# Two early loads of q asked for by ScalarE's queue instead of SyncE's, in a linear attention and gated MLP kernel

## The chip, the cores and the metric

The kernel runs on one core of a Trainium2 chip. The metric is the device time of one execution in microseconds, the median of several runs. The core has a matrix engine (TensorE, PE in the profile), VectorE (DVE), ScalarE (ACT), GpSimd (POOL), and SyncE (SP), which here does nothing but ask for transfers. ScalarE and GpSimd can ask for transfers too, each in a queue of its own. All transfers of the core run on its 16 DMA engines.

## The reference

Linear attention with decay in blocks of 64, and behind it a gated MLP with a spatial mix. B = 4, H = 8, S = 768, D = 64; the MLP has 512 inputs and 1024 hidden columns. Everything comes and goes as float32.

```
for b in range(nb):                        # blocks of 64 tokens
    intra = (qb @ kb.T * Dmask) @ vb       # Dmask = lam ** (i - j), i >= j
    inter = (qb * lam_pow) @ kv_state
    out[:, :, sl] = intra + inter
    kv_state = lam_block * kv_state + (kb * rev_pow).T @ vb
x = out as (B, S, 512)
h = relu(x @ w_in);  u, v = halves of h
v_n = (v - mean) / sqrt(var + 1e-6)
v_s = w_spatial @ v_n + b_spatial          # over the tokens
result = (u * v_s) @ w_out
```

## The kernel before, in words

The work goes in 12 steps, n = 0 to 11; three steps of 256 tokens make one batch element. Step n loads q, k and v of its 256 tokens for all 8 heads: one transfer of 512 KB each, which puts 128 partitions of 8 heads by 512 contiguous bytes in place. Each of q, k and v has three buffers, so step n takes the buffer of step n - 3.

The order of the work is written out by hand: the string ORDER lists tokens, and the loop at the end of the kernel turns each into the call of one helper. The last letter names the engine (T TensorE, D VectorE, A ScalarE, P GpSimd, S SyncE). Every engine works through its own tokens in the order of the string; waits between engines follow from the data. A token ahead of others on the same engine therefore holds these back for as long as it waits or works.

The tokens that matter here, with n the step:

- LK.n, LQ.n, LV.n load k, q and v. All go through the helper `load`, whose transfer is line 191 in the profile. `lam` loads the eight decay factors (L200). The argument 2 says all heads at once.
- WU runs matmuls on a constant tile, to keep TensorE busy (L212). LB, LN, LL, LX, LT make the decay tables from lam: a matmul (L217), a logarithm on ScalarE (L220), exponentials on ScalarE (L229 to L234). ScalarE loads a function table ahead of the logarithm and another ahead of the exponentials.
- KC.n and QC.n cast k and q to bf16 (L176 on VectorE, L178 on GpSimd). TK.n and TQ.n transpose them on TensorE (L328). EK.n copies the transposed k out of PSUM (L174), EQ.n does so for q and multiplies by its decay (L354).
- SC.n is the product of q and k (L369), MK.n masks it on VectorE (L373), VD.n multiplies v by its decay (L314), KV.n adds k times v to the state (L385), SS.n copies the state out (L174), AV.n forms the attention output (L406, L415), EX.n copies that out (L174).
- PV.n and PU.n are the two halves of the product with w_in (L438, L485). The later stages of the MLP are PW (L506), GB and GM (L511, L517), PO (L522).
- WI, WS and WO load the weights through GpSimd's queue, cast to bf16 on the way (L257, L262, L266). GT.0.1 makes GpSimd wait until k of step 1 has landed (L253), and WI.0, half of w_in, follows it. WI.1 stands behind half of VD.1 on GpSimd.

At the start SyncE's queue holds, in this order, k0, q0, k1, v0, q1, v1, k2, q2, v2, q3, k3, q4. ScalarE's queue holds lam alone; the next thing on ScalarE is the function table for the logarithm. On VectorE the casts, masks and products of the first steps come in the order QC.0, KC.1, EQ.0, VD.0 (two halves), MK.0 (two halves), EQ.1, MK.1. On TensorE the order is TQ.0, TK.0, TK.1, SC.0, KV.0.0, TQ.1, AV.0.0, SC.1.0, AV.0.1, SC.1.1, KV.0.1, KV.1.0, KV.1.1, AV.1.0, PV.0.1, AV.1.1, TK.2, TQ.2, with warm-up matmuls between.

Of the kernel before, what the change touches and what calls it, by code (L numbers as in the profile page):

```python
# [13 lines left out]


ORDER = """
LK.0.2.S lam.A pos.P LQ.0.2.S LK.1.2.S LV.0.2.S idn.P WU.-8.T LB.1.T msk.P LN.1.A LL.D LQ.1.2.S LX.A KC.0.2.P
LT.0.A LV.1.2.S QC.0.2.D mkc.A WU.29.T TQ.0.6.T LK.2.2.S TK.0.1.T GT.0.1.P WI.0.P KC.1.2.D EK.0.1.A EQ.0.6.D
WU.5.T TK.1.4.T LQ.2.2.S LT.1.A SC.0.1.5.T SC.0.0.1.T VD.0.0.D VD.0.1.D LV.2.2.S LT.2.A MK.0.0.1.D WU.7.T
KV.0.0.T QC.1.2.P MK.0.1.5.D EK.1.4.A WU.8.T TQ.1.2.T LQ.3.2.S SS.0.0.A AV.0.0.0.T EQ.1.2.D VD.1.0.P SY.0.0.A  # L20
# [564 lines left out]
```

## Time and profile before

| | |
|---|---|
| time, median of 3 runs | 148.21 us (147.82 to 151.35) |
| span of the profiled execution | 147.3 us |
| read from HBM, written | 24.77 MB, 6.29 MB |
| loads of q, k, v | 36, of 512 KB each |
| median time from issue to landing, k / q / v | 7.2 / 7.9 / 7.3 us |
| one issue in SyncE's queue, median for q | 1.74 us |
| half of w_in, from issue to landing | 8.9 and 10.1 us |
| lam's issue on ScalarE | 0.81 to 1.35 us |
| first function table on ScalarE | 1.38 us, 1.28 us long |

A line of the timeline gives the start, the duration, the engine, the source line, the operation with its output and inputs, and in brackets how long the engine had been idle before and what released it. "SPq" is an issue in SyncE's queue; its duration is the time for which the queue was held by that issue, and the data land later. In the table of stages each row is one stretch of time: its length, then for PE, PEld (the weight loads), DVE, ACT and POOL the busy time with the number of instructions, then the granted TensorE clock, the busy share of the DMA engines, and GB/s.

### The profile page before, as it was taken

Reading aid. Unit: us, or ns where it says so; the run is one execution under the profiler, and the core shown is the slowest. Engines: PE = TensorE matmul, PEld = TensorE weight load, DVE = VectorE, ACT = ScalarE, POOL = GpSimd, SP = SyncE. Lnnn points to the kernel's source line nnn. Section 1 sums busy time; section 2 is a strip of 40 time slices with the busy share of each in tenths; the row PEclk is TensorE's granted clock in tenths of the full one; section 3 lists DMA queues with packets and bytes.
Section 4 is the critical chain, followed back from the end, with each engine's and each line's share of the span. In section 5 each row is a group of like instructions: output and inputs, shape, how many; then the busy total and the mean of one; then the engine's idle time right before and its main releaser. Section 6 shows DMA issues by size and latency. Waiting matters only on the chain.

```text
span 147.3 us, 4874 instructions
## 1 busy us (share of the span) xinstructions
PE 138.3 (94%) x2075; PEld 90.7 (62%) x2075; DVE 101.1 (69%) x191; ACT 89.4 (61%) x167; POOL 70.5 (48%) x83
## 2 busy tenths in 40 slices
PE   6998698999999999899999899999999999999990
PEld 4786454768857768646656476556576565565540
DVE  1359606978996987799658499964598898738300
ACT  3979357968603876477994426676554567940370
POOL 7544660502269994864386924836735002034700
PEclk9999968999999999999999999999999999999998
DMA  3999999999999999999999998999993000070364
GB/s 87 302 290 260 270 256 258 217 238 293 276 287 283 291 268 176 304 259 95 277 324 180 200 237 260 312 200 346 255 219 97 2 7 0 0 268 21 142 259 169
DMA packets 54152, 31.25 MB, mean 212 GB/s; under 512 B 11634, under 2 KB 51058, under 8 KB 54130
## 3 DMA queue, kind: packets, MB, share of 16 engines
q1 hardware_dynamic: 51600, 28.05, 78.9%
q0 software_dynamic: 2384, 2.75, 11.0%
q8 instruction: 16, 0.26, 0.7%
q10 hardware_dynamic: 146, 0.13, 0.3%
q14 instruction: 6, 0.05, 0.1%
HBM read 24.77 MB, written 6.29 MB: 211 GB/s over the span
## 4 chain that ended last, share of the span: by engine, by line
PE 59%; DMA 19%; SPq 7%; POOL 5%; DVE 3%; ACT 2%; issue 2%; POOLq 0%; DVEq 0%; ACTq 0%
PE ps L506 15%; DMA q_in<-in_q_dram 14%; PE ps L522 12%; PE ps L485 11%; PE ps L438 10%; SPq L191 7%; DMA v_in<-in_v_dram 5%; POOL vd L314 3%; PE ps L415 2%; PE ps L369 2%; PE ps L385 2%; PE ps L498 1%; PE ps L328 1%; POOL qc L299 1%; PE ps L406 1%
## 5 line engine op out<-in xcount | busy, mean ns | idle before, releaser
L517 POOL TENSOR_TENSOR gT<-vsb,uT 128x384 bf16<-128x384 f32 x24 | 21.8, 920 | 31.1 <-DVE vsb L511 22.3
L506 PE MATMUL ps<-wt_sb,vn 128*128 128x384 bf16 x192 | 33.9, 326 | 0.0
L373 DVE TENSOR_TENSOR a_sb<-ps,m 128x1024 bf16<-128x1024 f32 x24 | 28.6, 1214 | 1.8 <-PE ps L369 1.4
L506 PEld LDWEIGHTS <-vn 128*128 128x128 bf16 x192 | 18.3, 98 | 11.9
L485 PE MATMUL ps<-xT,win_sb 128*128 128x256 bf16 x192 | 24.4, 273 | 0.0
L438 PE MATMUL ps<-win_sb,xT 128*128 128x512 bf16 x96 | 24.0, 387 | 0.0
L314 POOL TENSOR_TENSOR vd<-v_in,lv 128x512 bf16<-128x512 f32 x19 | 20.2, 1073 | 7.7 <-DMA v_in<-in_v_dram 7.7
L511 DVE TENSOR_TENSOR vsb<-ps,bsp 128x384 f32<-128x384 f32 x32 | 17.1, 549 | 8.6 <-PE ps L506 8.6
L522 PE MATMUL ps<-wout_sb,gT 128*128 128x512 bf16 x92 | 22.0, 379 | 0.0
L485 PEld LDWEIGHTS <-win_sb 128*128 128x128 bf16 x192 | 18.4, 98 | 4.9
L174 ACT ACTIVATE o_sb<-ps 128x512 f32<-128x512 f32 (+1 forms) x23 | 13.2, 587 | 11.1 <-PE ps L522 11.0
L174 ACT ACTIVATE xT<-ps 128x512 bf16<-128x512 f32 x22 | 15.2, 744 | 7.6 <-PE ps L415 7.6
L443 ACT ACTIVATE vh<-ps 128x512 bf16<-128x512 f32 x23 | 13.7, 597 | 9.1 <-PE ps L438 9.0
L453 DVE BATCH_NORM_STATS2 st<-vh 128x6 f32<-128x512 bf16 x24 | 16.3, 680 | 3.7 <-ACT vh L443 3.7
L299 POOL TENSOR_TENSOR qc<-q_in,lqn 128x512 bf16<-128x512 f32 x10 | 10.7, 1077 | 12.0 <-DMA q_in<-in_q_dram 9.0
L438 PEld LDWEIGHTS <-xT 128*128 128x128 bf16 x96 | 8.8, 98 | 9.6 <-issue 0.3
L522 PEld LDWEIGHTS <-gT 128*128 128x128 bf16 x92 | 8.8, 98 | 9.3
L443 ACT ACTIVATE uT<-ps 128x512 bf16<-128x512 f32 x20 | 11.7, 594 | 2.4 <-DVE mv L454 1.2
L178 POOL CAST kc<-k_in 128x1024 bf16<-128x1024 f32 x6 | 6.2, 1038 | 12.1 <-DMA k_in<-in_k_dram 7.8
L385 PE MATMUL ps<-vd,kc 64*64 64x64 bf16 x320 | 9.0, 194 | 2.6 <-ACT s_sb L174 1.0
L212 PE MATMUL ps<-warm 128*128 128x256 bf16 x61 | 9.7, 319 | 1.4 <-DVE warm L210 1.3
L174 ACT ACTIVATE kT<-ps 128x1024 bf16<-128x1024 bf16 x6 | 6.1, 1020 | 7.7 <-PE ps L328 7.2
(72 smaller groups left out, 178.0 us busy)
## 6 DMA issues: line engine op xcount, KB each, us to landing
k_in<-in_k_dram SPq DMA_DIRECT2D x12, 512.0 KB, 7.2
q_in<-in_q_dram SPq DMA_DIRECT2D x12, 512.0 KB, 7.9
v_in<-in_v_dram SPq DMA_DIRECT2D x12, 512.0 KB, 7.3
out_dram<-o_sb SPq DMA_DIRECT2D x23, 256.0 KB, 3.7
wsp_raw<-in_moe_w_spatial_dram POOLq DMA_DIRECT2D x2, 576.0 KB, 11.4
win_sb<-in_moe_w_in_dram POOLq DMA_DIRECT2D x2, 512.0 KB, 9.5
wout_sb<-in_moe_w_out_dram POOLq DMA_DIRECT2D x1, 512.0 KB, 8.9
bsp<-in_moe_b_spatial_dram SPq DMA_DIRECT2D x1, 384.0 KB, 6.7
```

The costliest lines, as they stand in the source:

```text
L174: nc.scalar.activation(out=o, in_=i, func=AF.Copy)
L299: vec(e).tensor_tensor(out=qc[n % NCA][:, :, :, o].rearrange("p u m d -> p (u m) d"), in0=q_in[n % NIN][:, 4 * o:4 * o + 4].rearrange("p u ...
L314: vec(e).tensor_tensor(out=vd[n % NCA].rearrange("p (o i w) m d -> p o i (w m) d", o=2, i=2)[o], in0=v_in[n % NIN].rearrange("p (o i w) m ...
L373: nc.vector.tensor_tensor(out=a_sb[n % NA][:, i].rearrange("p o w j x -> p (o w) (j x)"), in0=bank(b, 2).rearrange("p o (w y) -> p (o w) y ...
L438: nc.tensor.matmul(out=bank(b), lhsT=x[:, g % 2, c, c ^ (g // 2)], rhs=win_sb[:, g, DH:DFF], start=(g == 0), stop=(g == NCH - 1))
L443: nc.scalar.activation(out=o, in_=i, func=AF.Relu)
L453: nc.vector.bn_stats(out=st6[p2][:, t], in_=vh[p2][:, t])
L485: nc.tensor.matmul(out=pu[:, f2].rearrange("p (c x) -> p c x", c=2), lhsT=win_sb[:, g, f * P:(f + 1) * P], rhs=x[:, 4 * i + o:4 * i + 4 - ...
L506: nc.tensor.matmul(out=bank(b)[:, 0:HW], lhsT=vn[bb % 2][:, s, f * P:(f + 1) * P], rhs=wt_sb[:, s, i * HW:(i + 1) * HW], start=(s == 0), s ...
L511: nc.vector.tensor_tensor(out=vsb[(bb * 4 + f) % NVS][:, i * HW:(i + 1) * HW], in0=bank(b)[:, 0:HW], in1=bsp[:, i * HW:(i + 1) * HW], op=A ...
L517: vec(e).tensor_tensor(out=gT[bb % 2][:, f, cols], in0=vsb[(bb * 4 + f) % NVS][:, cols], in1=uT[bb % 2][:, f, cols], op=ALU.mult)
L522: nc.tensor.matmul(out=bank(b), lhsT=gT[bb % 2][:, f, t * P:(t + 1) * P], rhs=wout_sb[:, f, :], start=(f == 0), stop=(f == NCH - 1))
```

## The change

The loads of q of steps 0 and 1 leave SyncE's list and are put on ScalarE's, right behind the load of lam and ahead of everything else that ScalarE does. The aim is to have the first loads asked for from two queues at the same time. SyncE's queue then starts with k0, k1, v0, v1, k2, q2. No tile, size or computation changes; the lists of TensorE, VectorE and GpSimd stay as they are.

```
 ORDER = """
-LK.0.2.S lam.A pos.P LQ.0.2.S LK.1.2.S LV.0.2.S idn.P WU.-8.T LB.1.T msk.P LN.1.A LL.D LQ.1.2.S LX.A KC.0.2.P
+LK.0.2.S lam.A LQ.0.2.A LQ.1.2.A pos.P LK.1.2.S LV.0.2.S idn.P WU.-8.T LB.1.T msk.P LN.1.A LL.D LX.A KC.0.2.P
 LT.0.A LV.1.2.S QC.0.2.D mkc.A WU.29.T TQ.0.6.T LK.2.2.S TK.0.1.T GT.0.1.P WI.0.P KC.1.2.D EK.0.1.A EQ.0.6.D
```

## Prediction, made before the changed kernel was run

> **What bounds the kernel now.** I read the page first: busy shares, the 40 slices, the chain that ended last. TensorE is busy 94% of a 147.3 us span, and the transfer engines are full from the second slice on.
>
> ```profile
> PE 138.3 (94%) x2075; PEld 90.7 (62%) x2075; DVE 101.1 (69%) x191; ACT 89.4 (61%) x167; POOL 70.5 (48%) x83
> ...
> PEclk9999968999999999999999999999999999999998
> DMA  3999999999999999999999998999993000070364
> ```
>
> The reader should see two things: the DMA row is at 9 from 3.7 us to about 110 us, so a load cannot be made early without another coming late; and the TensorE clock drops once, near 20 us. Next I read the chain of waits, in order of time. Up to 22.6 us it is all loading; from 23.4 us it is TensorE, with only three later pieces of DMA.
>
> ```profile
> 6.81 1.74 SPq L191
> 8.59 1.74 SPq L191
> 10.37 12.22 DMA q_in<-in_q_dram
> 22.68 0.71 DVE qc L176
> 23.43 0.62 PE ps L328 x8
> ```
>
> So what counts for the end is when TQ.2 (the transposes of q of step 2, 23.43 us) can run, since behind it TensorE has hardly a gap. Then the timeline of the first 24 us, for the consumers of the first loads:
>
> ```profile
> 5.13 1.04 POOL L178 CAST kc<-k_in 128x1024 bf16<-128x1024 f32 x1 [0.43 <-DMA k_in<-in_k_dram]
> 6.90 0.69 DVE L176 CAST qc<-q_in 128x1024 bf16<-128x1024 f32 x1 [2.00 <-DMA q_in<-in_q_dram]
> 8.71 0.69 DVE L176 CAST kc<-k_in 128x1024 bf16<-128x1024 f32 x1 [1.11 <-DMA k_in<-in_k_dram]
> 10.52 1.29 DVE L314 TENSOR_TENSOR vd<-v_in,lv 128x512 bf16<-128x512 f32 x2 [0.52 <-DMA v_in<-in_v_dram]
> 12.37 1.03 POOL L178 CAST qc<-q_in 128x1024 bf16<-128x1024 f32 x1 [2.06 <-DMA q_in<-in_q_dram]
> 14.24 1.04 POOL L314 TENSOR_TENSOR vd<-v_in,lv 128x512 bf16<-128x512 f32 x1 [0.84 <-DMA v_in<-in_v_dram]
> ```
>
> Each waits for its transfer, so these are the landings of k0, q0, k1, v0, q1, v1: 5.1, 6.9, 8.7, 10.5, 12.4, 14.2 us, one every 1.8 us. The issues in SyncE's queue repeat every 1.78 us (5.03, 6.81, 8.59, 10.37): the queue runs at the pace of the transfers. The stage table shows that nothing is idle in it:
>
> ```profile
> 2.00:3.00 1.00, 1.00 (x6) 0.48 (x4) 0.00 (x0) 0.66 (x1) 0.94 (x3) 1.00 0.45 84
> 3.00:4.00 1.00, 1.00 (x5) 0.78 (x5) 0.01 (x1) 0.27 (x2) 0.88 (x4) 1.00 1.13 342
> 4.00:5.00 1.00, 1.00 (x6) 0.75 (x5) 0.89 (x3) 1.00 (x1) 0.68 (x1) 1.00 1.17 314
> 5.00:6.00 1.00, 1.00 (x7) 0.69 (x6) 0.00 (x0) 0.96 (x4) 0.86 (x1) 1.00 1.15 289
> ```
>
> The last two columns are the busy share of the transfer engines and GB/s: 289 to 342 GB/s from the fourth microsecond, with one queue in use.
>
> [...] one queue already fills the engines (289 GB/s). [...] No run here shows two load queues[...]. [...] granted clock 0.50 from 20 to 23 us, after TensorE was 0.25 to 0.52 busy between 16 and 19 us.
>
> **Part 1: what is removed and added in the queues.** Two issues leave SyncE's queue and two enter ScalarE's. Bytes, sizes and targets are the same. The gain in start is nil: the engines carry nothing before about 2.6 us either way (0.45 of the microsecond 2 to 3), and k0 alone then fills them. I price it at 0 to -0.2 us.
>
> **Part 2: the order of landing, worked out.** Unit: 1.8 us a load alone, 3.6 us while two share. k0 lands at 5.1, so its share of the stream starts at 3.3 on the scale of landings. q0 is asked for after lam's issue (0.81 + 0.54), some 0.6 us behind k0. k0 has a third done at 3.9; the rest at half rate takes 0.67 x 3.6 = 2.4: 6.3 us. q0 then lacks a third: 1.2 more, 7.5. k1, sharing with q1: 2.4 more, 9.9. q1: 1.2 more, 11.1. v0, now alone with 0.67 left: 1.2 more, 12.3. v1: 14.1. Against before: k0 +1.2, q0 +0.6, k1 +1.2, v0 +1.8, q1 -1.3, v1 -0.1. Bounds for v0: it cannot be later than the fifth landing, 12.4 (+1.9), and is 10.5 (0) if ScalarE's loads got nothing while SyncE's ran. I take +1.8. From v1 on the order and the bytes ahead are as before, so q2 keeps about 22.6 us. The half of w_in that GpSimd asks for at 9.39 waits for k1 and goes about 1.2 us later; this gives k2 and q2 a little, and its own first use (the matmuls of L438 at 19.42) moves later too.
>
> **Part 3: who waits for v0.** VectorE's list is KC.1, EQ.0, VD.0 (both halves), MK.0 (both), EQ.1, MK.1 (both). VD.0 at 10.52 moves to 12.3, and MK.0, 11.73 to 14.08, to 13.5 to 15.9. Behind it TensorE waits in program order: KV.0.0, TQ.1 (so that the earlier q1 buys nothing), AV.0.0 (14.01 to 15.8). EQ.1 follows MK.0 (14.18 to 16.0), then SC.1, MK.1, whose end goes from 18.05 to 19.85. AV.1.0 needs both masks. Before it ran at 18.87, 0.8 us after them, held by the state copies on ScalarE and by 0.76 us in which TensorE stood with no releaser. So after it runs between 19.85 (that slack used up) and 20.7 (all 1.8 passed on). From AV.1.0 to the end of TK.2 (22.83) TensorE took 3.96 us at the lowered clock, which gives 23.8 to 24.6 for the start of TQ.2, against 23.43 now, where it waits 0.6 us for q2. Shift at TQ.2: +0.4 to +1.2, middle +0.8.
>
> **Part 4: ScalarE.** Its table load (1.28 us, at 1.38) now stands behind two issues. The third issue of a queue cost 1.41 us in SyncE's, the second 0.56. Low end: 0.56 + 0.56, table load at 2.6, ready 3.9 against 3.71: +0.2 us. High end, [...]: ready at some 6.8, +3.1 us. I take about +1.0 (one of 0.56, one of 1.41). Behind it are the Ln, the Exps, the mask copies (end 8.03 to 9.0), then EK.0, which before waited 1.01 us for TensorE and now has its k0 later anyway. Even the high end puts EK.0's end at 12.1, ahead of the new MK.0 at 13.6, and EK.1 at 16.4 against EQ.1's end at 16.7. So it lies beside v0's delay: 0.
>
> **Part 5: how much reaches the end.** From 24 to 60 us TensorE has no idle time in the stage table (2.00 in each 2 us), so the shift goes through. Between 60 and 84 us it idles 0.41 + 0.06 + 0.07 + 0.38 = 0.9 us, for loads in the main; what of these isn't itself released later by the shifted work gives some back. Of +0.8 I let +0.7 remain: 148.2 + 0.7 = 148.9 us.
>
> **The rivals.** A, hidden: v0's delay ends in the wait for q2 (0.6 us) and the gaps of 0.9 us. For it: the sum of these exceeds 0.8. Against: the loads of the gaps follow the kernel's own releases. Time 148.2. B, faster: [...] the half-clock stretch is missed, or v0 is hardly late. Then the group of four L438 takes 0.97 for 1.66, TK.2 0.62 for 1.04, and with AV.1.1 some 1.2 us are saved; but TQ.2 still waits for q2, so at most the 0.6 us by which w_in's later transfer could bring q2 forward, and 0.2 of start: 147.4. C, slower: TensorE, starved from about 12 to 13.5 and 17 to 20 us, gets a second half-clock window of 3.4 us, in which half the work is lost (1.7 us), and ScalarE is at its high end, a further 0.5: 148.2 + 0.8 + 1.7 + 0.5 = 151.2, slower than before by 2%. For it: one such window is there already. Against: the warm-up matmuls fill the early gap.
>
> **How the numbers follow.** Forecast 0.55, A 0.2, B 0.1, C 0.15. The likeliest gives 148.9. The range goes from B less 0.3 for the spread of a time (147.82 to 148.21 in the two close runs), 147.1, up to C, 151.2, half of which lies beneath its own figure. Slower by 2% is 151.2 or more: most of C, 0.13. Faster by 2% is 145.2 or less, which no term here reaches: 0.03. Within: 0.84.
>
> **What would show it.** In the profile after: DVE's vd multiply at about 12.3 for 10.52, with the wait on v; GpSimd's cast of q1 near 11 for 12.37; the kc cast at 6.3; ScalarE's first table load between 2.6 and 5.5; TQ.2 at 23.8 to 24.6; DMA still at 9 in the second slice with no more GB/s. The prediction is wrong if v0 lands within 0.5 us of 10.5 (no equal sharing), if the rate in 3 to 14 us rises clearly over 290 GB/s, if TQ.2 moves and the end doesn't (Part 5), or if a new low-clock stretch shows.

## The result, and the profile after

The changed kernel takes 156.62 us (median; 155.68 to 157.28), the kernel before, with the later runs of it, 149.78 us (147.82 to 151.4). The ratio is 1.058, with a 95% interval of 1.048 to 1.068: slower by 5 to 7%, where 148.9 us was forecast with a range up to 151.2. (The ratios leave out slow executions, among them two of the kernel before at 151.4 us here and 10 of its 96 in four later series, at 155 to 157 us; none of these was profiled, so it isn't known whether they lose their time in the way that is shown below for the changed kernel.) The profiled executions span 147.3 us before and 154.0 us after.

The page of the changed kernel, busy shares and slices (one slice is 3.85 us):

```profile
PE 137.1 (89%) x2060; PEld 90.5 (59%) x2075; DVE 106.1 (69%) x191; ACT 89.9 (58%) x167; POOL 69.8 (45%) x83
...
PEclk9999998799999999999999999999999999999999
DMA  3999999999999969965999997999797000052364
```

TensorE does the same work (137.1 us busy for 138.3) in a span 6.7 us longer, so the loss is waiting. VectorE is busy 5.0 us longer than before with the same 191 instructions; some of them must have taken longer. The TensorE clock drops at a later place than before: it is 0.50 for 3.4 us from 25.5 us on, and was 0.50 for 3.4 us from 19.7 us on. The timeline of the changed kernel for the consumers of the first loads:

```profile
5.30 1.04 POOL L178 CAST kc<-k_in 128x1024 bf16<-128x1024 f32 x1 [0.65 <-DMA k_in<-in_k_dram]
7.56 0.69 DVE L176 CAST qc<-q_in 128x1024 bf16<-128x1024 f32 x1 [2.60 <-DMA q_in<-in_q_dram]
10.10 0.69 DVE L176 CAST kc<-k_in 128x1024 bf16<-128x1024 f32 x1 [1.85 <-DMA k_in<-in_k_dram]
11.97 1.03 POOL L178 CAST qc<-q_in 128x1024 bf16<-128x1024 f32 x1 [0.27 <-DMA q_in<-in_q_dram]
12.50 1.65 DVE L314 TENSOR_TENSOR vd<-v_in,lv 128x512 bf16<-128x512 f32 x2 [1.11 <-DMA v_in<-in_v_dram]
```

The order k0, q0, k1, q1, v0 came as forecast. The only number here that matters later is k1: 10.1 us instead of 8.7. The chain of waits of the changed kernel, the two stretches in which TensorE doesn't carry it (start, duration, what):

```profile
10.24 14.16 DMA q_in<-in_q_dram
24.49 0.70 DVE qc L176
25.25 0.82 PE ps L328 x8
...
32.04 2.03 POOL vd L314 x2
34.11 0.25 PE ps L385 x5
...
60.14 5.07 DVE gT L517
65.21 0.61 DVE st L453
```

The first stretch: q2 is there at 24.4 us for 22.6, and v2's multiply by its decay (VD.2) runs on GpSimd at 32.0 us. The second: one multiply on VectorE (GM, L517) takes 5 us. Neither was in the prediction. How late the work is after these, by the start of the same instruction before and after, in us:

| | before | after | later by |
|---|---|---|---|
| SC.2, scores of step 2 (L369) | 25.71 | 29.20 | 3.5 |
| KV.2, first use of v2 (L385) | 29.00 | 33.10 | 4.1 |
| first PU behind it (L485) | 29.71 | 34.69 | 5.0 |
| the multiply GM.0.3.0 (L517) | 54.94 | 60.05 | 5.1 |
| state product behind it (L385) | 59.65 | 67.78 | 8.1 |
| end of the span | 147.3 | 154.0 | 6.7 |

So 5 us come before 35 us, 3 more at 60 us, and 1.4 are given back.

**Why v2 is late.** The timeline of GpSimd, before: its request for half of w_in, the cast of k2, its request for w_spatial, VD.2.

```profile
9.39 0.92 POOL L257 DMA_DIRECT2D win_sb<-in_moe_w_in_dram  x1
...
19.53 1.04 POOL L178 CAST kc<-k_in 128x1024 bf16<-128x1024 f32 x1 [2.42 <-PE ps L415]
20.51 0.79 POOL L262 DMA_DIRECT2D wsp_raw<-in_moe_w_spatial_dram  x1
...
25.76 2.04 POOL L314 TENSOR_TENSOR vd<-v_in,lv 128x512 bf16<-128x512 f32 x2 [3.54 <-DMA v_in<-in_v_dram]
```

The same after:

```profile
10.78 0.92 POOL L257 DMA_DIRECT2D win_sb<-in_moe_w_in_dram  x1
...
18.61 1.04 POOL L178 CAST kc<-k_in 128x1024 bf16<-128x1024 f32 x1 [1.34 <-issue]
19.59 0.78 POOL L262 DMA_DIRECT2D wsp_raw<-in_moe_w_spatial_dram  x1
...
32.02 2.04 POOL L314 TENSOR_TENSOR vd<-v_in,lv 128x512 bf16<-128x512 f32 x2 [10.73 <-DVE a_sb L373]
```

The request for w_in, gated by k1, goes 1.4 us later, and that for w_spatial 0.9 us earlier: w_in's first packet now goes at 14.93 us for 13.12, when k2 is nearly through (whole at 16.02 us for 19.38), so the cast of k2 no longer waits for it and starts 0.9 us earlier. (The releaser of the last line is only the event that came last by the profile; the landing below tells what VD.2 waited for.) In the trace each load adds 16 counts to its semaphore, and the first use comes behind the last of them (v2's at 31.87 us, VD.2 at 32.02). I take each count for the part of the load that one of the 16 transfer engines has done. Landing of the 16 parts, in us:

```
        15 parts           last part
k2  before  17.99-18.36   19.38
    after   15.53-16.02 (all 16)
q2  before  19.79-20.19   22.59
    after   19.69-20.27   24.40
v2  before  23.59-25.45   25.61
    after   23.74-25.98   31.87
```

Fifteen parts of q2 and v2 come as before, within 0.1 and 0.5 us. One part is behind, by 1.8 us more for q2 and 6.3 us more for v2. (That it is the same engine's each time is assumed; the records don't name the engine.) What it runs into shows in the table of stages in half microseconds, the last column being GB/s. Before:

```profile
24.00:24.50 0.50, 0.50 (x4) 0.20 (x2) 0.41 (x1) 0.12 (x1) 0.00 (x0) 1.00 1.16 344
24.50:25.00 0.50, 0.50 (x4) 0.22 (x3) 0.50 (x2) 0.04 (x1) 0.00 (x0) 1.00 1.16 342
```

After:

```profile
24.00:24.50 0.50, 0.00 (x0) 0.00 (x0) 0.01 (x1) 0.47 (x1) 0.00 (x0) 1.00 1.22 297
24.50:25.00 0.50, 0.00 (x0) 0.00 (x0) 0.50 (x1) 0.00 (x0) 0.00 (x0) 1.00 1.17 220
```

At 340 GB/s SyncE's queue has the engines nearly alone (653 packets per us for 10 of GpSimd's queue, 24.0 to 25.0 us before); at 220 they share with the packets of GpSimd's queue (106 and 112 per us, 24.5 to 25.0 us after), which are cast on the way. Before, w_in's packets are through between 24.0 and 25.0 us but for some 10 per us, and w_spatial's first one goes at 24.99 us; in that gap the engine that is behind can catch up. After, w_spatial's first packet goes at 24.09 us, most of the gap is gone, and the engine does its part of v2 beside w_spatial. That it catches up in the gap isn't seen directly, but the rates fit. A load is 1024 packets of 512 bytes, 64 to a part if the parts are equal. Alone (10.5 to 12.5 us), SyncE's queue moves 575 packets per us in the kernel before, beside w_in (20.5 to 23.5 us) 138 of its own and 137 of GpSimd's, beside w_spatial (25.2 to 31.0 us) 107 and 107; its stream falls from 290 to 70 and 53 GB/s. At a sixteenth of these rates 64 packets take 1.8, 7.4 and 9.6 us, by estimate. v2's last part came 3.02 us after q2's before, so by the same estimate the engine was alone for some 1.4 us of it, and 7.47 us after it in the changed kernel, which leaves 0.5 us at most.

### The profile page after: what moved, and what is told of

The parts are those of the page before. It is cut to its first block, busy times and chain, and to the rows that moved or that the text cites. A ratio compares the mean times of both kernels' runs of the same rounds, so it can differ in the third digit from the quotient of the medians.

```text
span 154.0 us, 4860 instructions
## 1 busy us (share of the span) xinstructions
PE 137.1 (89%) x2060; PEld 90.5 (59%) x2075; DVE 106.1 (69%) x191; ACT 89.9 (58%) x167; POOL 69.8 (45%) x83
## 4 chain that ended last, share of the span: by engine, by line
PE 68%; DVE 10%; DMA 9%; SPq 6%; ACT 2%; issue 2%; POOL 1%; DVEq 0%
PE ps L506 19%; PE ps L522 13%; PE ps L438 11%; PE ps L485 10%; DMA q_in<-in_q_dram 9%; SPq L191 6%; DVE gT L517 3%; PE ps L369 3%; PE ps L415 3%; DVE a_sb L373 2%; PE ps L328 2%; PE ps L385 2%; PE ps L406 2%; PE ps L498 1%; POOL vd L314 1%
## 5 line engine op out<-in xcount | busy, mean ns | idle before, releaser
L517 POOL TENSOR_TENSOR gT<-vsb,uT 128x384 bf16<-128x384 f32 x24 | 21.8, 917 | 40.1 <-DVE vsb L511 31.4
L314 POOL TENSOR_TENSOR vd<-v_in,lv 128x512 bf16<-128x512 f32 x19 | 19.6, 1043 | 18.5 <-DVE a_sb L373 10.7
L485 PE MATMUL ps<-xT,win_sb 128*128 128x256 bf16 x192 | 24.4, 273 | 0.0
L522 PE MATMUL ps<-wout_sb,gT 128*128 128x512 bf16 x86 | 21.4, 379 | 0.4 <-issue 0.2
L485 PEld LDWEIGHTS <-win_sb 128*128 128x128 bf16 x192 | 18.4, 98 | 4.9
L385 PE MATMUL ps<-vd,kc 64*64 64x64 bf16 x320 | 8.9, 193 | 6.2 <-DVE s_sb L176 2.9
L385 PEld LDWEIGHTS <-kc 64*64 64x64 bf16 x320 | 7.4, 109 | 8.3 <-issue 7.3
L174 ACT ACTIVATE s_sb<-ps 128x256 bf16<-128x256 f32 x16 | 6.1, 382 | 8.3 <-PE ps L385 7.4
L415 PE MATMUL ps<-a_sb,vd 64*64 64x128 bf16 x384 | 10.5, 217 | 0.3 <-DVE a_sb L373 0.3
```

Source lines behind the costliest of these rows:

```text
L174: nc.scalar.activation(out=o, in_=i, func=AF.Copy)
L314: vec(e).tensor_tensor(out=vd[n % NCA].rearrange("p (o i w) m d -> p o i (w m) d", o=2, i=2)[o], in0=v_in[n % NIN].rearrange("p (o i w) m ...
L385: nc.tensor.matmul(out=pkv[row(o), u], lhsT=kc[n % NCA][row(c), u, m, o, :], rhs=vd[n % NCA][row(c), 4 * o + u, m, :], start=new and u == ...
L485: nc.tensor.matmul(out=pu[:, f2].rearrange("p (c x) -> p c x", c=2), lhsT=win_sb[:, g, f * P:(f + 1) * P], rhs=x[:, 4 * i + o:4 * i + 4 - ...
L517: vec(e).tensor_tensor(out=gT[bb % 2][:, f, cols], in0=vsb[(bb * 4 + f) % NVS][:, cols], in1=uT[bb % 2][:, f, cols], op=ALU.mult)
L522: nc.tensor.matmul(out=bank(b), lhsT=gT[bb % 2][:, f, t * P:(t + 1) * P], rhs=wout_sb[:, f, :], start=(f == 0), stop=(f == NCH - 1))
```

## The experiments

All compute the whole result. Where GpSimd is to be delayed, a token DL.n makes it fill a scratch tile of n columns that nothing reads (0.77 us for 768). Three theories stood at the start. Theory 1: w_in later, so k2 and w_spatial earlier, so the slowest part of q2 and v2 late. Theory 2: two queues of loads as such leave one transfer engine behind. Theory 3: v0 late, TensorE starved, half clock.

**e1: the changed kernel, with w_spatial asked for as late as before.**

```
-WS.1.P AV.1.1.3.T ...
+DL.768.P WS.1.P AV.1.1.3.T ...
```

> The changed kernel with 0.8 us of idle work on GpSimd ahead of its first request for w_spatial. Theory 1 (in the changed kernel k2 lands earlier, so GpSimd asks for w_spatial 0.9 us earlier, its packets close the gap in which SyncE's queue had the transfer engines alone, and the slowest engine's part of q2 and v2 comes late): the request goes from 19.6 to 20.4 us as before the change, q2 is there by 23.2 us for 24.5, v2 by 27 for 32.0, and the time comes down to 149 to 152 us. Theory 2 (two load queues at once leave one transfer engine behind the others, whatever w_spatial does) and theory 3 (v0 late, TensorE starved, half clock): 155 us or more, as the changed kernel.

Measured: 149.42 us, ratio to the kernel before 1.005 (1.001 to 1.009). Timeline of GpSimd and, below, the half microseconds of e1:

```profile
19.93 0.77 POOL L547 IOTA dly<- 128x768 int32 x1
20.66 0.79 POOL L262 DMA_DIRECT2D wsp_raw<-in_moe_w_spatial_dram  x1
...
25.74 2.04 POOL L314 TENSOR_TENSOR vd<-v_in,lv 128x512 bf16<-128x512 f32 x2 [3.37 <-DMA v_in<-in_v_dram]
```

```profile
24.00:24.50 0.50, 0.50 (x4) 0.24 (x3) 0.50 (x2) 0.50 (x1) 0.00 (x0) 1.00 1.14 338
24.50:25.00 0.50, 0.50 (x3) 0.15 (x2) 0.47 (x2) 0.50 (x2) 0.00 (x0) 1.00 1.16 344
```

So 0.8 us of idling on GpSimd takes away all but 0.5% of the loss. The gap at 24 to 25 us is back, v2 is whole at 25.59 us (and q2 at 22.02), and the multiply of L517 takes 0.55 us. Both queues of loads and the late v0 are still there, so theories 2 and 3 can hold for no more than the 0.5%, which is near the noise (e4 below has 0.4% with v0 on time).

**e2: the kernel before, with only w_in asked for later.** All loads stay in SyncE's queue in the old order.

```
-... GT.0.1.P WI.0.P KC.1.2.D ...
+... GT.0.1.P DL.768.P DL.512.P WI.0.P KC.1.2.D ...
```

> The kernel before with 1.4 us of idle work on GpSimd ahead of its first request for w_in, so that this goes out at 10.8 us as in the changed kernel; all loads stay in SyncE's queue. Theory 1: k2 lands some 2 us earlier, w_spatial is asked for earlier, v2 is there only after 30 us, 153 to 157 us. Theories 2 and 3: no second load queue and v0 on time, so 148 to 150.5 us.

Measured: 157.01 us, 1.0575 (1.0493 to 1.0657), the whole loss. GpSimd in e2:

```profile
9.27 1.38 POOL L547 IOTA dly<- 128x768 int32 x2
10.61 0.92 POOL L257 DMA_DIRECT2D win_sb<-in_moe_w_in_dram  x1
...
17.95 1.04 POOL L178 CAST kc<-k_in 128x1024 bf16<-128x1024 f32 x1 [0.96 <-PE ps L385]
18.92 0.79 POOL L262 DMA_DIRECT2D wsp_raw<-in_moe_w_spatial_dram  x1
...
31.93 2.04 POOL L314 TENSOR_TENSOR vd<-v_in,lv 128x512 bf16<-128x512 f32 x2 [11.30 <-DMA v_in<-in_v_dram]
```

Here the profile names v2's transfer as what VD.2 waited for. q2 is whole at 24.40 us and v2 at 31.78, as in the changed kernel (24.40 and 31.87): the later request for w_in is enough, with one queue and v0 on time.

**e3 and e4: the order without the second queue, and q0 alone in it.**

```
e3  -LK.0.2.S lam.A pos.P LQ.0.2.S LK.1.2.S LV.0.2.S ... LQ.1.2.S
    +LK.0.2.S lam.A pos.P LQ.0.2.S LK.1.2.S LQ.1.2.S LV.0.2.S ...
e4  -LK.0.2.S lam.A pos.P LQ.0.2.S LK.1.2.S LV.0.2.S ...
    +LK.0.2.S lam.A LQ.0.2.A pos.P LK.1.2.S LV.0.2.S ...
```

> All loads in SyncE's queue, in the order in which they land in the changed kernel (k0, q0, k1, q1, v0, v1); v0 lands at 12.4 us, but k1 at 8.7, so that w_in is asked for at 9.4 as before. Theory 1: the shift of v0 alone, 148 to 151 us. Theory 2: as before, 148 to 150. Theory 3: all of the loss, 154 to 157 us.

> Half of the change: q0 in ScalarE's queue, q1 in SyncE's where it was. k0 lands near 6.3 us, k1 near 8.9, v0 near 10.5. Theory 1: w_in is asked for at some 9.6 us, 148 to 151 us. Theory 2: a good part of the loss, 151 to 155. Theory 3: 148 to 150.

Measured: e3 149.33 us, 1.0053 (0.9998 to 1.0107); e4 149.32 us, 1.0039 (0.9992 to 1.0087). In both k1 comes in time, w_in is asked for at 9.36 and 9.42 us, w_spatial at 20.50 and 20.51, and v2 is whole at 25.40 and 25.67. One load of q in ScalarE's queue did no measurable harm here, where k1 wasn't pushed back. In e3 v0 is late (12.27 us) about as in the changed kernel, in e4 on time (10.52 us); the times don't tell the two apart, so no cost of a late v0 is seen.

**e5: the changed kernel, with w_in freed from k1.** Its gate is q0 instead, and a delay puts the request at 9.20 us.

```
-... GT.0.1.P WI.0.P KC.1.2.D ...
+... GT.1.0.P DL.1024.P WI.0.P KC.1.2.D ...
```

> The changed kernel, with its first request for w_in at the time that it had before (9.4 us for 10.8): GpSimd waits for q0 in place of k1 and then does 1.1 us of idle work. Both load queues stay. Theory 1 (w_in later, so k2 earlier, so w_spatial earlier, so v2's last part late): k2 lands near 19 us again, w_spatial is asked for at 20.4 or later, v2 is there by 27 us, 148 to 151 us. A rival, that the two queues are needed for the loss too: 153 us or more.

Measured: single times of 148.92, 148.88, 153.04 and 157.57 us; no ratio can be given. In the profiled one (148.92) w_spatial is asked for at 20.30 us and v2 is whole at 27.45. With the request at its old time the loss can be avoided, but not in each execution. That v2 is caught in some and not in others is argued from this profile; the other times have none. How far the engine is behind counts too: in e7 below w_spatial is asked for earlier than here, at 20.07 us, and v2 is still whole at 25.14 us; there q2's last part was there at 20.73 us, here at 23.52.

**e8: half the delay of e2** (DL.640, 0.65 us, in the same place).

> The kernel before with 0.7 us of idle work ahead of the first request for w_in, half of that of the changed kernel. If the loss grows with the lateness: about 152 us. If it is a cliff, since k2 either comes ahead of w_in's packets or is caught in them: either 148 to 149.5, or 156 to 157. Theory 1 names the sign in the trace: k2's landing goes with w_spatial's request, and the time with v2's last part.

Measured: 150.88, 156.94, 157.09 and 159.83 us, no ratio. In the profiled one (150.88) 15 parts of k2 are there by 15.8 us and the last at 19.1; w_spatial goes at 20.23, v2 is whole at 29.0. One of the four lies near 151, three near 157 and above: more like a cliff than a slope. In this profile the multiply of L517, at 58.5 us, takes 0.55 us; the collision that is told of below, under e6, isn't there. That it makes the step from 151 to 157 is possible, and not shown.

**e9: the kernel before, with w_spatial asked for earlier.** w_in and all loads are untouched; the cast of k2 (KC.2) now stands behind the two requests.

```
-... KV.1.1.T KC.2.2.P AV.1.0.3.T ... / WS.1.P AV.1.1.3.T EV.0.1.5.A QC.2.2.D GT.2.1.P WS.0.P TK.2.2.T ...
+... KV.1.1.T DL.1024.P DL.768.P WS.1.P GT.2.1.P WS.0.P KC.2.2.P AV.1.0.3.T ... / AV.1.1.3.T EV.0.1.5.A QC.2.2.D TK.2.2.T ...
```

> The kernel before with its loads and w_in untouched; only the two requests for w_spatial are taken ahead of the cast of k2 on GpSimd and set by idle work to about 18.9 and 19.8 us, where the delayed w_in had put them (20.5 and 21.4 before). q2 has its usual 22.5 to 23.2 us, since w_in is as before. If the early w_spatial alone makes v2's last part late: v2 after 29 us and 151 to 156 us, less than the 157 of the delayed w_in since q2 is on time. If it takes w_in's lateness too: v2 by 27 us, 148 to 150 us.

Measured: 158.27 us, 1.0589 (1.048 to 1.0698), more than expected. GpSimd and TensorE in e9:

```profile
18.83 0.79 POOL L262 DMA_DIRECT2D wsp_raw<-in_moe_w_spatial_dram  x1
...
31.69 2.04 POOL L314 TENSOR_TENSOR vd<-v_in,lv 128x512 bf16<-128x512 f32 x2 [10.10 <-DMA v_in<-in_v_dram]
```

```profile
25.94 0.64 PE L369 MATMUL ps<-qT,kT 64*64 64x128 bf16 x32
...
32.79 0.31 PE L385 MATMUL ps<-vd,kc 64*64 64x64 bf16 x8 [3.49 <-POOL vd L314]
```

q2 is whole at 22.82 us and the scores of step 2 start at 25.94, as before the change (25.71); v2 is whole at 31.55 us, and TensorE waits for VD.2. The cast of k2 runs at 20.54 us for 19.53, which can account for no more than these 0.2 us. So the time of w_spatial is enough, and v2 alone makes the delay.

**e10: the changed kernel, kept warm while q2 is missing.** Twelve warm-up matmuls (WU.12) ahead of TQ.2.

> The changed kernel with twelve warm-up matmuls between the transposes of k2 and q2, where TensorE stood 2.5 us for q2 and then ran at half clock from 25.5 to 28.9 us. If the half clock is a part of the loss of its own: the granted clock stays at 1.00, the score matmuls of step 2 start at some 28 us for 29.2, and 0.5 to 1.7 us come back, 155 to 156. If v2, which lands after 31 us, decides behind it anyway: 156 to 157.5, no gain.

Measured: 156.50, 157.55, 159.49 and, once, 149.33 us. TensorE, and one microsecond of the stages, in the profiled execution (156.50 us):

```profile
26.62 0.64 PE L369 MATMUL ps<-qT,kT 64*64 64x128 bf16 x32
...
32.43 0.31 PE L385 MATMUL ps<-vd,kc 64*64 64x64 bf16 x8 [2.45 <-POOL vd L314]
```

```profile
27.00:28.00 1.00, 1.00 (x24) 0.51 (x13) 0.96 (x3) 0.98 (x2) 0.00 (x0) 1.00 1.16 219
```

The column before the last two is the granted clock: 1.00, where the changed kernel has 0.50. The scores move 2.6 us forward (29.20 to 26.62), KV.2 only 0.7 (33.10 to 32.43), and the span stays (154.8 us). In this execution, half clock and the late q2 lie in the shadow of v2. The one of 149.33 us has no profile.

**e6 and e7: the multiply of L517.** In the changed kernel it takes 5.15 us, against 0.55. VectorE and GpSimd at that place in the changed kernel:

```profile
60.05 5.15 DVE L517 TENSOR_TENSOR gT<-vsb,uT 128x384 bf16<-128x384 f32 x1
```

```profile
59.89 1.04 POOL L299 TENSOR_TENSOR qc<-q_in,lqn 128x512 bf16<-128x512 f32 x1
60.89 1.03 POOL L314 TENSOR_TENSOR vd<-v_in,lv 128x512 bf16<-128x512 f32 x1
61.89 1.03 POOL L299 TENSOR_TENSOR qc<-q_in,lqn 128x512 bf16<-128x512 f32 x1
62.89 1.03 POOL L314 TENSOR_TENSOR vd<-v_in,lv 128x512 bf16<-128x512 f32 x1
63.89 0.90 POOL L517 TENSOR_TENSOR gT<-vsb,uT 128x384 bf16<-128x384 f32 x1
```

The multiply starts 0.16 us behind the first of five operations of GpSimd and ends 0.41 us behind the last. GpSimd has no gap between the five. In e2 it is the same with four of them: the multiply takes 4.12 us, from 0.20 us behind the start of the first (62.14 us) to 0.42 us behind the end of the last (66.04 us). That GpSimd's operations held the multiply back is read from these times; the record names no releaser. Before, the multiply ran at 54.94 us, and GpSimd had a gap there, from 54.99 to 57.19 us, waiting for q7:

```profile
54.94 0.55 DVE L517 TENSOR_TENSOR gT<-vsb,uT 128x384 bf16<-128x384 f32 x1
```

```profile
57.19 1.04 POOL L299 TENSOR_TENSOR qc<-q_in,lqn 128x512 bf16<-128x512 f32 x1 [2.20 <-DMA q_in<-in_q_dram]
```

With the program 5 us later, q7 has already landed and the gap is missing. e6 and e7 move this one multiply to GpSimd (GM.0.3.0.D to GM.0.3.0.P), in the changed kernel and in the one before.

> The changed kernel with one multiply (L517, batch 0, third group, first half), which took 5.15 us on VectorE at 60 us while GpSimd ran five operations without a gap, moved to GpSimd's list. If this wait is a second part of the loss of its own: the span between the transposes of step 3 and the end is as before the change, and 1.5 to 3 us come back, 153.5 to 155 us. If it is only idle time that would have been spent in another wait: within 0.7 us of the changed kernel, 156 to 157.

> The same move in the kernel before, as a control; there the multiply took 0.55 us on VectorE with GpSimd idle beside it. It costs GpSimd 0.9 us ahead of two multiplies that wait for q7 anyway: 148 to 149.3 us.

Measured: e6 151.85 us, 1.021 (1.008 to 1.034); e7 148.76 us, 1.0055 (1.002 to 1.009). v2 is still late in e6 (31.32 us). The stage from 64 to 68 us, in which TensorE loses the time, in the changed kernel and then in e6:

```profile
64.00:66.00 2.00, 0.86 (x6) 0.40 (x4) 1.97 (x4) 0.62 (x2) 0.79 (x1) 1.00 1.15 305
66.00:68.00 2.00, 0.22 (x15) 0.22 (x17) 1.97 (x6) 0.00 (x0) 0.00 (x0) 1.00 0.79 207
```

```profile
64.00:66.00 2.00, 2.00 (x77) 1.42 (x77) 1.33 (x3) 1.30 (x4) 1.56 (x3) 1.00 1.15 318
66.00:68.00 2.00, 1.95 (x59) 1.24 (x50) 1.65 (x2) 1.15 (x2) 1.75 (x3) 1.00 0.61 154
```

TensorE works 1.08 of 4 us there, and 3.95 with the multiply moved. By the profiled spans the collision costs 3.1 us (154.0 - 150.9), by the medians, which come from different series, 4.8 (156.62 - 151.85): about half of the loss. In the kernel before the move gains nothing.

**e11 and e12: is there more to be had from the gap?** e11 asks for w_spatial 0.38 us later in the kernel before; e12 adds 0.65 us ahead of the second half of w_in.

> The kernel before with 0.4 us of idle work ahead of the first request for w_spatial: a little more room between w_in's packets and w_spatial's. If that room is already enough in the kernel before: 148 to 149.3 us, as before. If its slower single runs come from a v2 caught now and then: these go and the median falls by up to 0.7 us.

> An attempt at a faster version out of the finding: the kernel before, with 0.6 us of idle work ahead of the second half of w_in and 0.4 us ahead of w_spatial, so that the transfer engine that is behind finds room for q2 and for v2 between GpSimd's transfers. q2's last part lands by 22 us for 22.9, v2 by 26. If the gain of up to 0.6 us in the wait for q2 reaches the end: 147 to 148 us, 0.2 to 0.6% faster. If the later weights cost it again (w_in's second half is first used at 27 us, w_spatial at 35 us) or the engines' order behind it takes it up: 148 to 149.5.

Measured: e11 148.36 us, 0.993 (0.984 to 1.003), which is not told apart from no change; e12 148.77 us, 1.000 (0.997 to 1.004). q2 in e12 is whole at 21.09 us instead of 22.59, and v2 at 25.36: nothing of it reaches the end. No version was faster than the kernel before by more than the noise.

## Why the prediction was wrong, by its own steps

**Part 1, right.** With two queues the engines moved 288 GB/s from 5 to 6 us, for 289 before. No start was gained, and none lost.

**Part 2, the landings: right in order, two sizes off.** Forecast 6.3, 7.5, 9.9, 11.1, 12.3 us for k0, q0, k1, q1, v0; measured 5.3, 7.56, 10.1, 11.97, 12.50. q0 hardly slowed k0, so 1.0 of the 1.2 us of delay counted for it was not there; q1 came 0.9 us later than sharing by halves gave. Halves were an assumption: no run before had shown two queues of loads. From 6 to 10 us, where both had work, SyncE's queue moved 1224 packets and ScalarE's 1046; from 4.5 to 5.5 us, with k0 all but through, they moved 14 and 560.

**Part 2, the last two sentences: the step that failed.** "From v1 on the order and the bytes ahead are as before, so q2 keeps about 22.6 us", and the later w_in "gives k2 and q2 a little". The order within SyncE's queue is as before, but not what runs beside it. I had the delay of w_in (forecast 1.2 us, measured 1.4) and followed it to w_in's own matmuls only. The earlier k2 that I counted as a small gift let GpSimd go on to its next request: w_spatial 0.92 us earlier, no gap for the engine that lags, v2 whole at 31.9 us for 25.6. The runs show that w_in's time alone makes the loss (e2), that w_spatial's time alone makes it (e9), and that putting w_spatial back takes it away (e1); what happens on the one engine in between is read from landings and rates. I also treated a landing as one moment and one rate; the table of parts above has one part up to 5.9 us behind the next to last (31.87 - 25.98).

**Part 3, right up to AV.1.0, wrong behind it, and hidden.** v0 moved to 12.5 us and AV.1.0 from 18.87 to 20.20, within the 19.85 to 20.7 forecast. From there to the end of TK.2 the sum kept the lowered clock of the kernel before (3.96 us). In the changed kernel that half-clock stretch is missing, which was a term of rival B, with TensorE 0.44 to 0.48 busy from 18 to 20 us. The rows of the table of stages, before and after:

```profile
21.00:22.00 1.00, 1.00 (x28) 0.83 (x28) 0.00 (x0) 0.69 (x2) 1.00 (x3) 0.50 1.19 222
```

```profile
21.00:22.00 1.00, 0.95 (x27) 0.46 (x26) 0.00 (x0) 0.24 (x2) 0.29 (x1) 1.00 1.19 216
```

TK.2 is done at 22.75 us for 22.83, so v0's delay was used up there by luck of the clock. In the changed kernel TQ.2 then started at 25.25 us, outside 23.8 to 24.6, because of q2's last part; in e1, where q2 came at 22.02, it started at 22.92, ahead of the 23.43 of before. The 0.7 us forecast for the end are near the 0.5% of e1 and e3, but no run shows that v0 makes them.

**Part 4, right in its cost.** The table load moved to 2.48 us, and the logarithm behind it from 3.71 to 3.77: of the 1.0 us counted, 0.06 came, and it costs nothing at the end. (The high end of 3.1 us was an estimate, from issues of 0.56 and 1.41 us at twice the time.)

**Part 5, half right.** That TensorE has no slack from 24 to 60 us was right, and for this reason a 5 us delay got through whole. That a shift passes through unchanged was wrong: at 60 us it met GpSimd in another phase and grew by 3 us (e6), before 1.4 us were given back.

**The rivals.** C had the direction and the half clock, which came at 25.5 to 28.9 us, 3.4 us as counted; but the clock was not the cause (e10). Its sum of 151.2 us had no term for a transfer on GpSimd's queue. A, v0's delay hidden, is nearest to what e1 and e3 show: in e3 TQ.2 waits 1.55 us for q2, as A has it, and starts at 23.74 us; in e1 the full clock has made the delay good by then. B's missing half-clock stretch came, and v2 outweighed it.

**What stays open.** Why one engine is behind the other fifteen, and why by so much more in some executions. It is behind before q2 comes: in 12 of 14 profiles the last part of w_in's first half lags the next by 0.8 to 1.5 us, and q2's last part follows that lag, at 20.7 to 21.1 us where it is 0.2 to 0.3, 22.0 to 22.9 where it is 0.8 to 1.0, and 23.5 to 24.4 where it is more. The later w_in doesn't settle it: the changed kernel and e1 ask for w_in at nearly the same time and have q2 at 24.40 and 22.02 us. Nor does w_spatial: in the changed kernel its first packet goes at 24.09 us, when q2 is all but through. In all the profiles a packet of instructions, 16 KB and 0.9 to 1.2 us long, starts between 14.4 and 16.0 us; the records don't say which engine it or a lag is on. It fits, and is argued only. Moving that packet was not tried.

## What to carry to other kernels

When a load moves, follow every request that is gated by it on other engines, and ask what each will then run beside; a request that comes earlier can do more harm than one that comes late (here w_spatial 0.9 us earlier, with v2 6.3 us later). Where a second queue with other packets joins, look at the slowest of a load's 16 parts, and not only at the mean rate (v2's last part came 5.9 us behind the next to last). A shift of the whole program is not neutral (5.1 us grew to 8.1 here): check which pairs of VectorE and GpSimd operations were apart only because GpSimd was waiting.

## What the runs showed that I had not expected

- Two queues got the same number of packets (138 and 137 per us beside w_in, 107 and 107 beside w_spatial) and very unequal bytes and time: SyncE's loads, in packets of 512 bytes, fell from 290 to 70 and 53 GB/s beside packets recorded with 1024 and 1536 bytes.
- GpSimd's requests moved their first packet 3.7 to 4.8 us after they were issued (9.39 to 13.12, 10.78 to 14.93, 15.23 to 20.02 us). A gap in the traffic was thus set by what GpSimd had done some 4 us earlier.
- A VectorE multiply of 0.55 us took 5.15 us beside five back-to-back GpSimd operations (4.1 to 4.4 us in e2, e9 and e10).
- 0.9 us in the time of one request went with 6.7 us in the span, and 0.8 us of idling (e1) undid all but 0.5% of the loss.
